# Softmax weights and q of two slots in two PSUM banks, six banks left for matmuls, GpSimd subtractions beside every large VectorE product, and the bound written by ScalarE

## The chip, the cores and the metric

The kernel runs on one core of a Trainium2 chip (trn2). The metric is the device time of one execution in microseconds; the median of three runs of the kernel before is 639.03 us.

## The reference

The input is one sequence of 2048 tokens with 640 features. Two branches of it are mixed by a gate per token.

```python
# A: 32 heads of 20 features, each token attends to 8 positions, 2 apart
logits = einsum("bhsd,bhswd->bhsw", q, k_gathered) * scale      # w = 8 offsets 0, 2, .., 14 back
logits = where(position >= 0, logits, -1e9)
a = (softmax(logits) @ v_gathered) @ wo
# B: 640 -> 1728 -> 640 with Mish between
b = mish(x @ w1 + b1) @ w2
g = sigmoid((x * gate_w).sum(-1))
out = g * a + (1 - g) * b
```

All is float32. Each float32 matrix is split into a high part (rounded to the type that TensorE multiplies, `fp32r`) and a low part (the rest), and a product is three matmuls: high by high, high by low, low by high.

## The kernel before, in words

**Stages on TensorE.** TensorE runs one fixed series: nine warm-up matmuls; eight units of q, k and v (`qkv`: a quarter of the heads and half of the tokens each, 8 slots of 15 matmuls) with the first MLP layer (`mlp1`: 52 tiles of 15 matmuls) between them; the second MLP layer (`mlp2`) as seven products a, b, c, e, g, d, f in Strassen's manner, each over seven blocks `kc` of the inner dimension; and `wo_out`, four token blocks of five output tiles. A product of `mlp2` has four to six output tiles ("p0", "u0" and so on, for two halves P), each with a PSUM bank of its own. Its first two and its last two blocks are done tile by tile: six matmuls for one tile, then six for the next.

**Splits.** Each operand is loaded into a staging buffer (`raw`, `hb`), ScalarE writes its high part (line 337), and VectorE or GpSimd subtracts it to give the low part (`low` in `split`, line 340). A `pair` holds both. TensorE waits for ScalarE before the first matmul of a pair, and for the subtracting engine before the second.

**Attention** runs on VectorE: for each two slots a product of q and the windows of k (line 424), a sum over the 20 features (line 427), the softmax (lines 442 to 452, with the exponential on ScalarE), then a product of weights `pw` and the windows of v (line 458) and sums (463, 464, 466). For the first tokens, which have positions before the start, GpSimd adds a bound of -BIG to one partition of the logits (line 435).

**What sets the order.** Nothing is issued as it comes. `Plan.run` plays all tasks through a list of assumed durations and writes the instructions of each engine in the order in which they start there; on the chip each engine works its list strictly in that order and waits at semaphores. Tasks marked "ANY" (most subtractions) may go to either engine. VectorE takes one only if it is due: if TensorE comes to it within `NEAR` = 8000 ns of the plan. GpSimd takes one while attention runs only if it ends within the time `quiet` in which VectorE does a large task of a certain kind, and is then bound by a wait (`follow`) to the VectorE instruction before that one. Before the change the kind is the sum "qk sum" alone (line 427). Banks of PSUM are handed out in a ring (`ps_buf`, 8 of them); a new tile takes the bank of the tile eight before it.

Of the kernel before, what the change touches and what calls it, by code (L numbers as in the profile page):

```python
# [26 lines left out]
BIG = 1e9  # L27
# [31 lines left out]
class Plan:  # L59
# [18 lines left out]
    def add(self, eng, ns, fn, after=(), rank=0.0, take=(), hold=(), size=0, kind="", late=0):  # L78
        t = Task(eng, ns, fn, rank, size / 330.0)
        t.kind, t.late = kind, late  # L80
        if eng == "POOL" and type(ns) is not tuple:
            t.ns = (ns, ns)
        for p in after:
            if p is not None:
                p.then.append(t)
                t.waits += 1
        t.take = list(take)
        t.hold = list(take) + [b for b in hold if b not in take]
        for b in t.hold:
            b.left += 1  # L90
        self.tasks.append(t)
        return t

    def run(self):
        ready = {e: [] for e in self.LAG}
# [33 lines left out]
        while left:  # L129
            again = not events or events[0][0] > now  # L130
            while again:
                again = False
                for e in self.LAG:
                    if busy[e]:
                        continue
                    fit = [t for t in ready[e] if fits(t)]
                    on = begun and loud
                    if e == "POOL":
                        fit += [t for t in shared if fits(t)]
                        if on:  # L140
                            fit = [t for t in fit if now + t.ns[0] <= quiet + 150 or t.rank < 0]
                    elif e == "DVE":
                        fit += [t for t in shared if fits(t) and (not on or due(t))]
                    if not fit:
                        continue
                    t = min(fit, key=lambda t: t.key)
                    if t.both:
                        shared.remove(t)
                        t.eng = e
                    else:  # L150
                        ready[e].remove(t)
                    if type(t.ns) is tuple:
                        t.ns = t.ns[e == "DVE"]
                    for b in t.take:
                        b.ring.free -= 1
                        b.ring.at += 1
                        b.t = b.make()
                    t.start = now
                    ins = t.fn(e) if t.both else t.fn()
                    if e == "POOL" and on and quiet > now and gate and ins:  # L160
                        self.follow(ins, gate)
                    if e == "DVE":
                        if t.kind:
                            begun = True
                            loud -= 1
                        if t.kind == "qk sum":
                            quiet, gate = now + t.ns, last
                        last = ins or last
                    if e == "PE":
                        begun_pe = max(begun_pe, t.pos)  # L170
                    busy[e] = again = True
                    end = over = now + t.ns * self.CARE.get(e, 1.0)
                    heapq.heappush(events, (over, n, "idle", e))
                    if t.land:
                        wire = max(wire, end) + t.land
                        end = wire + (0 if e == "SP" else self.ADDING)
# [36 lines left out]
def kernel(ctx: ExitStack, tc: tile.TileContext, x, wq, wo, w1, b1, w2, xt, gw, out):  # L213
    nc = tc.nc
    scale = DH ** -0.5
    V, G, A = nc.vector, nc.gpsimd, nc.scalar

    keep = ctx.enter_context(tc.tile_pool(name="keep", bufs=1))
    dram = ctx.enter_context(tc.tile_pool(name="dram", bufs=1, space=DRAM))
    psum = ctx.enter_context(tc.tile_pool(name="psum", bufs=8, space=PSUM))  # L220
    pe = ctx.enter_context(tc.tile_pool(name="pe", bufs=1, side="right"))
    at = ctx.enter_context(tc.tile_pool(name="at", bufs=1))

    NPAIR, NW, NRAW, NH = 21, 3, 7, 4
    def follow(ins, gate):
        tc.add_manual_dep(ins.ins, gate.ins.name,
                          mybir.DependencyInfo(mybir.DependencyClass.Sync, mybir.DependencyReason.DATA), reason="beside")

    plan = Plan({"bank": 8, "pair": NPAIR, "w": NW, "raw": NRAW, "raw1": 1, "hb": NH,
                 "ot": 1, "b": 11}, follow)  # L230

    def ps_buf():
        return plan.buf("bank", lambda: psum.tile([128, 512], F32, name="bank"))

    def pair_buf():
        return plan.buf("pair", lambda: pe.tile([128, 2, 512], F32R, name="pair", bufs=NPAIR))
# [34 lines left out]
    add = plan.add  # L271
# [5 lines left out]

    A.preload_act_table_set("mish")
    bias = keep.tile([128, FC + 1], F32)
    bound = keep.tile([1, 7, 7], F32)  # L280
    zt = keep.tile([128, 2, 8], F32)
    gate = keep.tile([128, 2, 8], F32)
    gc = keep.tile([128, 2, 8], F32)
# [18 lines left out]

    lg = at.tile([128, 8, HQ, W], F32, name="lg")
    lg_w = lg.rearrange("p s h w -> p s w h")
    pw = at.tile([128, 8, W, HQ], F32, name="pw")
    pr = at.tile([128, 2, W, QF], F32, name="pr")
    mx = at.tile([128, 8, HQ], F32, name="mx")
    sm = at.tile([128, 8, HQ], F32, name="sm")
# [15 lines left out]
    def consts_g():  # L324
        for i in range(2):
            G.memset(KV[i][0:1, 0:7], 0.0)

        G.memset(bound, 0.0)
        G.affine_select(bound, bound, pattern=[[1, 7], [1, 7]], compare_op=OP.is_ge,
                        fill=-BIG / scale, base=-7, channel_multiplier=0)  # L330

    cg = add("POOL", 5000, consts_g, rank=-1)


# [60 lines left out]
    def window(kv, s0, which):  # L395
        a = kv[:, s0:s0 + 9, which, :]
        return bass.AP(tensor=a.tensor, offset=a.offset, ap=[list(a.ap[0]), [ROW, 2], [ROW, W], [1, QF]])

    freed = {}
    spilled = {}  # L400
    att_end = {}
    shared_out = {}

    def attention(u, P, hq, ready, gates):


        kv, q = KV[UNIT[u]], Q[UNIT[u]]
# [13 lines left out]

        def scores(s0, rank, after):
            def mul():
                return V.tensor_tensor(pr, window(kv, s0, 0), q[:, s0:s0 + 2, None, :].to_broadcast([128, 2, W, QF]), op=OP.mult)  # L424

            def red():
                V.tensor_reduce(lg_w[:, s0:s0 + 2], pr.rearrange("p s w (h d) -> p s w h d", d=DH), op=OP.add, axis=AX.X)  # L427

            step = chain(rank)
            step("DVE", 2850, mul, ready[s0] + after, kind="qk")  # L430
            return step("DVE", 2750, red, kind="qk sum")

        def bounded(a, b, after):
            b = min(b, 7)
            return add("POOL", 3400, lambda: G.tensor_tensor(lg[0:1, a:b, :, 0:7], lg[0:1, a:b, :, 0:7],  # L435
                       bound[:, a:b, None, :].to_broadcast([1, b - a, HQ, 7]), op=OP.add), [cg] + after, rank=-1)

        def softmax(a, rank, after):

# [633 lines left out]
```

## Time and profile before

| | |
|---|---|
| three runs | 640.16, 639.03, 638.97 us; median 639.03 |
| profiled execution | span 636.9 us from its first to its last instruction; its time outside the span is not shown |
| TensorE busy | 631.9 us, 99% |
| VectorE busy | 584.1 us, 92% |
| ScalarE, GpSimd busy | 277.4 us, 215.2 us |

The median is 2.1 us longer than the span of the profiled execution, which is what starting and ending an execution takes outside it. The busy share of an engine is an average over stages; the list of waits says who ended the idle time of each engine, and the chain that ended last says which engine's work the end of the span hangs on.

### The profile page before, as it was taken

The numbers are of one execution on the slowest core, as the hardware profiler recorded it, in microseconds if no ns is written. First come the engines' busy times: TensorE is split into PE (matmuls) and PEld (weight loads), VectorE is DVE, ScalarE is ACT, GpSimd is POOL, SyncE is SP. The second block draws the span as 40 slices with busy tenths as digits, with TensorE's granted clock in tenths as the row PEclk, the third lists the DMA queues.
The fourth block names the chain that finished last, engine by engine and source line by source line (L and its number), as shares of the span: only waits on it lengthen the run. The fifth ranks groups of instructions, "written<-read, shape, count | busy, mean of one in ns | idle before, by whom it ended". The sixth has DMA issues, their size and how long they took to land.

```text
span 636.9 us, 8494 instructions
## 1 busy us (share of the span) xinstructions
PE 631.9 (99%) x2805; PEld 526.2 (83%) x2805; DVE 584.1 (92%) x584; ACT 277.4 (44%) x565; POOL 215.2 (34%) x157
## 2 busy tenths in 40 slices
PE   9999999999999999999999999999999999999997
PEld 6888888888888888888888888888888888888886
DVE  7888999999999999999899989799999999999941
ACT  7553353435436332542524244584676426721100
POOL 2212313131414442132343423204107328967310
PEclk9999999999999999999999999999999999999999
DMA  9999998867954994798499955989996758844642
GB/s 327 373 283 180 190 263 227 229 174 223 296 172 86 271 258 93 222 218 178 84 245 214 219 122 147 254 274 282 312 286 220 226 159 288 289 155 149 193 158 82
DMA packets 91323, 137.26 MB, mean 216 GB/s; under 512 B 12128, under 2 KB 41184, under 8 KB 91216
## 3 DMA queue, kind: packets, MB, share of 16 engines
q1 hardware_dynamic: 83600, 122.83, 62.6%
q0 software_dynamic: 7680, 13.90, 14.8%
q8 instruction: 22, 0.36, 0.2%
q14 instruction: 21, 0.17, 0.1%
HBM read 77.11 MB, written 57.81 MB: 212 GB/s over the span
## 4 chain that ended last, share of the span: by engine, by line
PE 99%; DVE 0%; issue 0%
PE bank L374 33%; PE bank L372 33%; PE bank L373 33%; PE bank L510 1%; PE bank L319 1%; DVE kvq L954 0%; DVE lg L315 0%
## 5 line engine op out<-in xcount | busy, mean ns | idle before, releaser
L372 PE MATMUL bank<-pair 128*128 128x512 f32 (+1 forms) x476 | 183.8, 386 | 0.0
L374 PE MATMUL bank<-pair 128*128 128x512 f32 (+1 forms) x476 | 183.7, 386 | 0.0
L373 PE MATMUL bank<-pair 128*128 128x512 f32 (+1 forms) x476 | 183.7, 386 | 0.0
L373 PEld LDWEIGHTS bank<-pair 128*128 128x128 f32 x476 | 89.3, 188 | 17.2
L374 PEld LDWEIGHTS bank<-pair 128*128 128x128 f32 x476 | 89.4, 188 | 17.1
L372 PEld LDWEIGHTS bank<-pair 128*128 128x128 f32 x476 | 89.3, 188 | 17.0
L424 DVE TENSOR_TENSOR pr<-kvq 128x2560 f32<-128x2560 f32 x32 | 90.8, 2839 | 3.5 <-DMA kvq<-kvq 1.6
L337 ACT ACTIVATE pair<-raw 128x512 fp32r<-128x512 f32 (+3 forms) x122 | 72.0, 615 | 48.4 <-DMA raw<-o 21.5
L458 DVE TENSOR_TENSOR pr<-kvq,pw 128x2560 f32<-128x2560 f32 x32 | 91.1, 2848 | 0.9
L427 DVE TENSOR_REDUCE lg<-pr 128x128 f32<-128x2560 f32 x32 | 90.2, 2818 | 0.6
L516 ACT ACTIVATE kvq<-bank 128x320 f32<-128x320 f32 x64 | 28.3, 442 | 114.7 <-PE bank L374 114.7
L435 POOL TENSOR_TENSOR lg<-lg,bound 1x168 f32<-1x168 f32 (+1 forms) x16 | 68.8, 4303 | 20.4 <-DVE lg L427 18.7
L625 ACT ACTIVATE hb<-bank,bias 128x512 f32<-128x512 f32 x52 | 35.9, 690 | 90.7 <-PE bank L374 77.2
L374 PE MATMUL bank<-pair,kvq 128*128 128x512 f32 (+1 forms) x188 | 72.6, 386 | 0.0
L372 PE MATMUL bank<-pair,kvq 128*128 128x512 f32 (+1 forms) x188 | 72.6, 386 | 0.0
L373 PE MATMUL bank<-pair,kvq 128*128 128x512 f32 (+1 forms) x188 | 72.6, 386 | 0.0
L340 POOL TENSOR_TENSOR pair<-raw,pair 128x496 fp32r<-128x496 f32 (+2 forms) x31 | 42.6, 1386 | 86.4 <-ACT pair L337 30.0
L372 PE MATMUL bank<-pair,w 128*128 128x512 f32 x182 | 70.8, 389 | 0.0
L373 PE MATMUL bank<-pair,w 128*128 128x512 f32 x182 | 70.8, 389 | 0.0
L374 PE MATMUL bank<-pair,w 128*128 128x512 f32 x182 | 70.8, 389 | 0.0
L340 DVE TENSOR_TENSOR pair<-raw,pair 128x512 fp32r<-128x512 f32 (+1 forms) x91 | 63.9, 721 | 5.2 <-ACT pair L337 5.2
L337 ACT ACTIVATE pair<-hb 128x512 fp32r<-128x512 f32 (+3 forms) x63 | 38.8, 615 | 42.7 <-DMA hb<-o 16.0
(89 smaller groups left out, 873.9 us busy)
## 6 DMA issues: line engine op xcount, KB each, us to landing
actt<-hb SPq DMA_DIRECT2D x52, 256.0 KB, 4.6
act<-hb SPq DMA_DIRECT2D x38, 256.0 KB, 4.6
raw<-actt SPq DMA_DIRECT2D x32, 256.0 KB, 4.5
raw<-act SPq DMA_DIRECT2D x29, 256.0 KB, 4.0
actt<-hb POOLq DMA_DIRECT2D x26, 256.0 KB, 6.2
actt<-actt POOLq DMA_DIRECT2D x24, 256.0 KB, 5.4
hb<-actt SPq DMA_DIRECT2D x24, 256.0 KB, 4.5
kvq<-in_xt SPq DMA_DIRECT2D x16, 320.0 KB, 7.2
```

Source lines behind the costliest of these rows:

```text
L319: nc.tensor.matmul(warm_bank.t, idle[:, :128], idle, start=True, stop=True)
L337: a = add("ACT", act_ns(n), lambda: A.activation(hi(), raw(), AF.Copy), after, rank=rank, take=take, hold=hold)
L340: return (V if e == "DVE" else G).tensor_tensor(lo(), raw(), hi().bitcast(F32), op=OP.subtract)
L372: nc.tensor.matmul(ps, ah, bh, start=first, stop=False, skip_group_check=more)
L373: nc.tensor.matmul(ps, ah, bl, start=False, stop=False, skip_group_check=more)
L374: nc.tensor.matmul(ps, al, bh, start=False, stop=last, skip_group_check=more)
L424: return V.tensor_tensor(pr, window(kv, s0, 0), q[:, s0:s0 + 2, None, :].to_broadcast([128, 2, W, QF]), op=OP.mult)
L427: V.tensor_reduce(lg_w[:, s0:s0 + 2], pr.rearrange("p s w (h d) -> p s w h d", d=DH), op=OP.add, axis=AX.X)
L435: return add("POOL", 3400, lambda: G.tensor_tensor(lg[0:1, a:b, :, 0:7], lg[0:1, a:b, :, 0:7], bound[:, a:b, None, :].to_broadcast([1, b - ...
L458: V.tensor_tensor(pr.rearrange("p s w (h d) -> p s w h d", d=DH), vw, pw[:, s0:s0 + 2, :, :, None].to_broadcast([128, 2, W, HQ, DH]), op=O ...
L516: a = add("ACT", 330, lambda: A.activation(kv[:, 7 + s], ps.t[:, QF:3 * QF].rearrange("p (a b) -> p a b", a=2), AF.Copy), [done] + before, ...
L625: a = add("ACT", 595, lambda: A.activation(to(it()), src(), AF.Mish, bias=bias[:n, fc:fc + 1]), after + [bias_in], rank=NEXT, take=[] if h ...
```

## The change

The weights `pw` and a copy `qs` of q for two slots each get a PSUM bank; ScalarE makes the copy (line 431 after) when the product before it has been done. So both large products of attention read one operand from PSUM and one from SBUF. Six banks are left for matmuls. The planner lets GpSimd work beside all three large kinds ("qk", "qk sum", "pv"). The bound is no longer added by GpSimd but written over the logits by ScalarE, slot by slot (line 440 after, 3 or 4 instructions where one was).

```diff
-                        if t.kind == "qk sum":
+                        if t.kind:
                             quiet, gate = now + t.ns, last
...
-    psum = ctx.enter_context(tc.tile_pool(name="psum", bufs=8, space=PSUM))
+    NBANK = 6
+    psum = ctx.enter_context(tc.tile_pool(name="psum", bufs=1, space=PSUM))
...
-        return plan.buf("bank", lambda: psum.tile([128, 512], F32, name="bank"))
+        return plan.buf("bank", lambda: psum.tile([128, 512], F32, name="bank", bufs=NBANK))
...
-    pw = at.tile([128, 8, W, HQ], F32, name="pw")
+    pw = psum.tile([128, 8, W, HQ], F32, name="pw")
+    qs = psum.tile([128, 512], F32, name="qs")[:, :2 * QF].rearrange("p (s f) -> p s f", f=QF)
...
-        G.memset(bound, 0.0)
-        G.affine_select(bound, bound, pattern=[[1, 7], [1, 7]], compare_op=OP.is_ge,
-                        fill=-BIG / scale, base=-7, channel_multiplier=0)
+        G.memset(bound, -BIG / scale)
...
-                return V.tensor_tensor(pr, window(kv, s0, 0), q[:, s0:s0 + 2, None, :].to_broadcast([128, 2, W, QF]), op=OP.mult)
+                return V.tensor_tensor(pr, window(kv, s0, 0), qs[:, :, None, :].to_broadcast([128, 2, W, QF]), op=OP.mult)
...
-            step("DVE", 2850, mul, ready[s0] + after, kind="qk")
+            c = add("ACT", 360, lambda: A.activation(qs, q[:, s0:s0 + 2], AF.Copy), ready[s0] + [asked[0]], rank=-1)
+            asked[0] = step("DVE", 2850, mul, [c] + after, kind="qk")
...
-            return add("POOL", 3400, lambda: G.tensor_tensor(lg[0:1, a:b, :, 0:7], lg[0:1, a:b, :, 0:7],
-                       bound[:, a:b, None, :].to_broadcast([1, b - a, HQ, 7]), op=OP.add), [cg] + after, rank=-1)
+            def run():
+                for s in range(a, b):
+                    A.activation(lg[0:1, s, :, 0:7 - s], bound[:, :, 0:7 - s], AF.Copy)
+            return add("ACT", 220 * (b - a), run, [cg] + after, rank=-1)
```

Since the planner's rule and its tasks change, the whole order is written anew. TensorE's list has the same matmuls in the same series, 924 of each of the three lines. Of the subtractions of line 340, VectorE had 165 and now has 120, GpSimd had 44 and now has 89. Lines 704, 808 and 821 (710, 814 and 827 after) share their tasks a little differently.

The first place is on VectorE where product c ends and product e begins. Line 808 (814 after) adds the four banks of c, one by one, to a kept tile; `pr` and `lg` belong to attention. Before:

```order
L340 TENSOR_TENSOR pair_4085<-raw_4013,pair_4085 128x512 [waits DMAHW5_49,PE_49,Activation_49]
L340 TENSOR_TENSOR pair_4102<-hb_4025,pair_4102 128x512 [waits DMAHW7_49,Activation_49]
L340 TENSOR_TENSOR pair_4108<-raw_4041,pair_4108 128x512 [waits DMAHW0_49,Activation_49]
L340 TENSOR_TENSOR pair_4119<-hb_4047,pair_4119 128x512 [waits DMAHW1_49,Activation_49]
L808 TENSOR_TENSOR kvq1_213<-kvq1_213,bank_3982 128x512 [waits PE_49]
L340 TENSOR_TENSOR pair_4122<-raw_4058,pair_4122 128x512 [waits DMAHW3_49,DMAHW2_49,Activation_49]
L340 TENSOR_TENSOR pair_4133<-raw_4088,pair_4133 128x512 [waits DMAHW4_49,Activation_49]
L808 TENSOR_TENSOR kvq1_213<-kvq1_213,bank_3999 128x512 [waits PE_49]
L340 TENSOR_TENSOR pair_4141<-hb_4091,pair_4141 128x512 [waits DMAHW5_49,Activation_49]
L808 TENSOR_TENSOR kvq1_213<-kvq1_213,bank_4017 128x512 [waits PE_49]
L808 TENSOR_TENSOR kvq1_213<-kvq1_213,bank_4034 128x512 [waits PE_49]
```

And the same place after:

```order
L425 TENSOR_TENSOR pr_218<-kvq2_3263,qs_217 128x2560
L340 TENSOR_TENSOR pair_4201<-raw_4073,pair_4201 128x512 [waits DMAHW2_49,DMAHW3_49,PE_49,Activation_49]
L340 TENSOR_TENSOR pair_4209<-raw_4082,pair_4209 128x512 [waits DMAHW4_49,PE_49,Activation_49]
L814 TENSOR_TENSOR kvq1_213<-kvq1_213,bank_4062 128x512 [waits PE_49]
L814 TENSOR_TENSOR kvq1_213<-kvq1_213,bank_4076 128x512 [waits PE_49]
L814 TENSOR_TENSOR kvq1_213<-kvq1_213,bank_4092 128x512 [waits PE_49]
L814 TENSOR_TENSOR kvq1_213<-kvq1_213,bank_4102 128x512 [waits PE_49]
L428 TENSOR_REDUCE lg_215<-pr_218 128x2x8x8 [waits DVE_49]
L340 TENSOR_TENSOR pair_4247<-raw_4114,pair_4247 128x512 [waits DMAHW6_49,Activation_49]
L340 TENSOR_TENSOR pair_4249<-hb_4166,pair_4249 128x512 [waits DMAHW5_49,Activation_49]
```

Before, the subtractions of the first blocks of e stand ahead of the four additions; now two of them stand behind the additions and behind a sum of attention.

The second place is TensorE's list at the same point: the last matmul of c and the first ones of e, the second of which (pair_4247, pair_4108 before) is block `kc` = 1 for the first tile. Before:

```order
L374 MATMUL bank_4034<-pair_4068,pair_4038 128x512
L372 MATMUL bank_4183<-pair_4085,pair_4076 128x512 [waits Activation_49]
L373 MATMUL bank_4183<-pair_4085,pair_4076 128x512 [waits DVE_49]
L374 MATMUL bank_4183<-pair_4085,pair_4076 128x512
L372 MATMUL bank_4183<-pair_4108,pair_4076 128x512 [waits Activation_49]
L373 MATMUL bank_4183<-pair_4108,pair_4076 128x512 [waits DVE_49]
```

And after:

```order
L374 MATMUL bank_4102<-pair_4195,pair_4097 128x512
L372 MATMUL bank_4234<-pair_4209,pair_4201 128x512 [waits Activation_49]
L373 MATMUL bank_4234<-pair_4209,pair_4201 128x512 [waits DVE_49]
L374 MATMUL bank_4234<-pair_4209,pair_4201 128x512
L372 MATMUL bank_4234<-pair_4247,pair_4201 128x512 [waits Activation_49]
L373 MATMUL bank_4234<-pair_4247,pair_4201 128x512 [waits DVE_49]
```

TensorE's series has not moved; the wait for VectorE in the last row is five matmuls behind the last matmul of c in both.

The third place is GpSimd in the first quarter of the program, where weights of q, k and v (128x496) are split; line 613 (619 after) is a DMA that adds to a block in DRAM. Before:

```order
L613 DMA actt_1_1_127<-hb 128x512 [waits DMAHW3_49,Activation_49]
L340 TENSOR_TENSOR pair<-raw,pair 128x496 [waits DMAHW6_49,DVE_49]
L340 TENSOR_TENSOR pair<-raw,pair 128x496 [waits DMAHW7_49,Activation_49]
L613 DMA actt_0_2_121<-hb 128x512 [waits DMAHW4_49,Activation_49]
L613 DMA actt_1_2_128<-hb 128x512 [waits DMAHW7_49,Activation_49]
L340 TENSOR_TENSOR pair<-raw,pair 128x496 [waits DMAHW0_49,DVE_49]
L340 TENSOR_TENSOR pair<-raw,pair 128x496 [waits DMAHW2_49,PE_49]
L435 TENSOR_TENSOR lg<-lg,bound 1x24x7 [waits DVE_49]
```

And after:

```order
L340 TENSOR_TENSOR pair<-raw,pair 128x496 [waits DMAHW3_49,DVE_49,Activation_49]
L340 TENSOR_TENSOR pair<-raw,pair 128x496 [waits DMAHW4_49,Activation_49]
L619 DMA actt_1_1_127<-hb 128x512 [waits DMAHW0_49,Activation_49]
L340 TENSOR_TENSOR pair<-raw,pair 128x496 [waits DVE_49,DMAHW5_49,PE_49,Activation_49]
L710 TENSOR_TENSOR raw<-raw 128x256 [waits DMAHW7_49,DMAHW1_49,Pool_49]
L340 TENSOR_TENSOR pair<-raw,pair 128x496 [waits DVE_49,DMAHW2_49,PE_49,Activation_49]
L340 TENSOR_TENSOR pair<-raw,pair 128x496 [waits DMAHW5_49,PE_49,Activation_49]
```

All five subtractions of this quarter's weights are now GpSimd's, with the adding DMAs between them, and the addition of the bound is gone from its list.

More of the change, by code (lines that the diff above doesn't have):

```diff
@@ L227, in follow @@
                           mybir.DependencyInfo(mybir.DependencyClass.Sync, mybir.DependencyReason.DATA), reason="beside")
-    plan = Plan({"bank": 8, "pair": NPAIR, "w": NW, "raw": NRAW, "raw1": 1, "hb": NH,
+    plan = Plan({"bank": NBANK, "pair": NPAIR, "w": NW, "raw": NRAW, "raw1": 1, "hb": NH,
                  "ot": 1, "b": 11}, follow)
     def ps_buf():
-        return plan.buf("bank", lambda: psum.tile([128, 512], F32, name="bank"))
+        return plan.buf("bank", lambda: psum.tile([128, 512], F32, name="bank", bufs=NBANK))
     def pair_buf():
@@ L279 @@
     bias = keep.tile([128, FC + 1], F32)
-    bound = keep.tile([1, 7, 7], F32)
+    bound = keep.tile([1, HQ, 7], F32)
     zt = keep.tile([128, 2, 8], F32)
@@ L399 @@
     freed = {}
+    asked = [None]
     spilled = {}
```

## The prediction

> **What bounds the kernel now.** I read the page first: busy times, the clock row, and the chain that ended last.
>
> ```profile
> PE 631.9 (99%) x2805; PEld 526.2 (83%) x2805; DVE 584.1 (92%) x584; ACT 277.4 (44%) x565; POOL 215.2 (34%) x157
> PEclk9999999999999999999999999999999999999999
> PE 99%; DVE 0%; issue 0%
> ```
>
> TensorE is busy for 631.9 us of a span of 636.9 at a full clock, and the chain is TensorE's nearly alone. A busy engine may still be spaced out by waits, so the list of waits for TensorE comes next, and then the end of the timeline.
>
> ```profile
> PE bank L319 <- DVE lg L315: 1.2, 1, 1.2
> ...
> 632.52 0.39 PE L373 MATMUL bank<-pair,kvq 128*128 128x512 f32 x1
> 632.74 0.39 PE L374 MATMUL bank<-pair,kvq 128*128 128x512 f32 x1
> 633.17 0.69 DVE L954 TENSOR_TENSOR kvq<-bank,kvq 128x512 f32<-128x512 f32 x1 [2.71 <-PE bank L374]
> 633.89 0.33 SPq L346 DMA_DIRECT2D out<-kvq  x1
> ```
>
> In the whole span TensorE waits once, for 1.2 us before its first matmul. From there it runs without a gap to 632.74. What lies outside is those 1.2 us and some 4 us at the end: the last addition and the last transfer. So there is nothing to win on TensorE: every microsecond that VectorE saves is saved beside TensorE, and every microsecond for which TensorE is made to wait is added to the end whole, since no gap can take it up. The question is only whether the new order makes it wait.
>
> **The change part by part.** First the engines beside TensorE. These rows, from the groups with shapes kept apart, price the moved work.
>
> ```profile
> L340 DVE TENSOR_TENSOR pair<-raw,pair 128x512 fp32r<-128x512 f32 x76 | 54.7, 736 | 5.2 <-ACT pair L337 5.2
> L340 POOL TENSOR_TENSOR pair<-raw,pair 128x512 fp32r<-128x512 f32 x13 | 18.3, 1413 | 36.4 <-ACT pair L337 21.1 <-DVE pr L424 11.5 <-DVE pair L340 3.8
> L435 POOL TENSOR_TENSOR lg<-lg,bound 1x224 f32<-1x224 f32 x8 | 42.9, 5358 | 19.1 <-DVE lg L427 17.6 <-PE bank L374 1.6
> L435 POOL TENSOR_TENSOR lg<-lg,bound 1x168 f32<-1x168 f32 x8 | 26.0, 3248 | 1.2 <-DVE lg L427 1.1
> L516 ACT ACTIVATE kvq<-bank 128x320 f32<-128x320 f32 x64 | 28.3, 442 | 114.7 <-PE bank L374 114.7
> L520 ACT ACTIVATE hx<-bank 128x16 f32<-128x16 f32 x64 | 12.7, 198 | 0.0
> ```
>
> VectorE loses 45 subtractions: 45 x 0.736 = 33 us, so some 551 us stay of 584.1. GpSimd gains them at 45 x 1.413 = 64 us and loses the bound, 42.9 + 26.0 = 69 us: no change in sum. ScalarE gains 32 copies of 320 elements, 32 x 0.442 = 14 us, and 56 short writes at 0.198 us, 11 us: 302 us. None of these comes near TensorE's 631.9, so as sums they cost nothing. If their cover were gone, it would have to be by a delay at one place.
>
> The large products keep their length if an operand in PSUM costs what one in SBUF costs. Additions of the same size with and without a bank show it:
>
> ```profile
> L808 DVE TENSOR_TENSOR kvq<-kvq,bank 128x512 f32<-128x512 f32 x8 | 5.3, 672 | 0.0
> L808 DVE TENSOR_TENSOR kvq<-kvq 128x512 f32<-128x512 f32 x4 | 2.6, 677 | 0.0
> ```
>
> 672 against 677 ns: nothing, so both products stay at their present length. A gain of those 5 ns on 64 products would be 0.3 us; a loss, were it even 0.1 us each, 6.4 us, and both lie beside TensorE.
>
> **The ring of six banks.** In the stages with q, k and v a tile takes 15 matmuls of about 0.227 us (632.52 to 632.74, and finer 469.54 to 469.77 below), 3.4 us, so the bank of the tile six before it has five tiles, 17 us, to be read out. ScalarE reads it, and its longest hold-up is here:
>
> ```profile
> 70.95 0.66 ACT L628 ACTIVATE hb<-hb 128x512 f32<-128x512 f32 x1
> 76.22 0.74 ACT L337 ACTIVATE w<-raw 128x640 fp32r<-128x640 f32 x1 [4.61 <-DMA raw<-in_w]
> 79.82 0.62 ACT L337 ACTIVATE pair<-raw 128x496 fp32r<-128x496 f32 x1 [2.85 <-DMA raw<-in_wq]
> 80.34 0.42 ACT L516 ACTIVATE kvq<-bank 128x320 f32<-128x320 f32 x1
> ```
>
> No bank is read from 71 to 80.3 us, 9.4 us, which fits into 17. ScalarE's new instructions are a new wait, too: the copy of q waits for the product before, the bound for a sum, and behind them stand the readers of banks and the high parts. Such a wait is at most one VectorE product, 2.8 us, and fits as well: 9.4 + 2.8 = 12.2. I take nothing here. In `mlp2` tiles are finished 6 x 0.227 = 1.36 us apart, and the third tile of e, the first to reuse a bank of c, starts five such steps, 6.8 us, after that bank is full; the additions that empty them stand directly in turn, so nothing here either.
>
> **The place that costs.** I followed each subtraction of the new order from TensorE's wait back through its engine's list to the last instruction ahead of it that itself waits for a late matmul. One place fails, where product c ends. These are the matmuls and the VectorE rows there before.
>
> ```profile
> 469.54 0.39 PE L374 MATMUL bank<-pair 128*128 128x512 f32 x1
> 469.77 0.39 PE L372 MATMUL bank<-pair 128*128 128x512 f32 x1
> ...
> 466.52 0.69 DVE L340 TENSOR_TENSOR pair<-raw,pair 128x512 fp32r<-128x512 f32 x1
> 470.73 1.28 DVE L808 TENSOR_TENSOR kvq<-kvq,bank 128x512 f32<-128x512 f32 x2
> ```
>
> The matmul at 469.54 is the last of c. The fifth after it, at 469.54 + 5 x 0.227 = 470.67, needs the low part of the second pair of e. Before, that subtraction ran at 466.52 and was done at 467.21, 3.5 us early, and the fourth addition of c's banks came long after it. In the new order the same subtraction (pair_4247) stands behind the four additions and behind a sum of attention (line 428), and the fourth addition waits for that last matmul. So TensorE waits for a chain that its own matmul starts:
>
> ```profile
> 527.84 2.81 DVE L427 TENSOR_REDUCE lg<-pr 128x128 f32<-128x2560 f32 x1
> 530.57 0.68 DVE L340 TENSOR_TENSOR pair<-hb,pair 128x512 fp32r<-128x512 f32 x1
> ...
> 89.08 2.83 DVE L424 TENSOR_TENSOR pr<-kvq 128x2560 f32<-128x2560 f32 x1 [1.06 <-DMA kvq<-kvq]
> 92.00 2.47 POOL L340 TENSOR_TENSOR pair<-raw,pair 128x496 fp32r<-128x496 f32 x2 [13.22 <-DVE pr L424]
> ```
>
> From the start of the matmul to the addition: 633.17 - 632.74 = 0.43 us, as at the end of the span. The addition: 0.60, half the distance from 470.73 over two of them. The sum of attention: 530.57 - 527.84 = 2.73. The subtraction: 0.68. From its end to the engine that waits: 92.00 - 91.91 = 0.09, by the GpSimd row that waited for a product. Together 4.53 us. Of these TensorE covers five matmuls, 1.13 us. It waits 4.53 - 1.13 = 3.4 us. Lower end 3.1 (no hand-over time, a slightly shorter start); upper end 4.5, if VectorE comes a little late to its first addition. The next subtraction (pair_4249) is wanted 12 matmuls later, 2.7 us, and is done 0.6 us after the first: no second wait.
>
> Behind the place nothing takes the 3.4 us back, as TensorE has no gap. Everything beside it only gets that much more time. The other parts being nothing, the span becomes 636.9 + 3.4 = 640.3, and with the 2.1 us that lie around the span of the profiled execution, 642.4, which is 0.5% above the median of 639.03. A measurement of this kernel tells about 0.2%, 1.28 us, from no change.
>
> **The rivals.** *A second wait, on GpSimd's list.* Twice as many subtractions stand there now, with the adding DMAs of line 613 among them.
>
> ```profile
> POOL actt L613 <- DMA actt<-actt: 45.8, 9, 7.6
> POOL actt L613 <- ACT hb L625: 20.7, 3, 11.4
> ```
>
> The longest single holds are 7.6 and 11.4 us. A subtraction that is 3.5 us early, as the one above, and is held by 7.6, costs 4.1: 646.5. For it: GpSimd takes 1.41 us where VectorE takes 0.74. Against: before, 44 subtractions stood in that list and none made TensorE wait, and these adding DMAs are mostly over before `mlp2`, where the margins are short. The Trainium skill's GPSIMD Engine Reference (Engine selection) advises VectorE for elementwise work on two inputs, since GpSimd is about 2x slower there; the ratio 1413 to 736 agrees. That rule speaks against the change and raises this rival's chance, no more. I give it 0.2, together with a late load at the place above, which would give 643 to 646.
>
> *The products shut GpSimd out after all.* GpSimd stands still beside VectorE instructions with two SBUF operands; here beside a product and sums, while an addition with a bank passes:
>
> ```profile
> 530.79 25.72 POOL L435 TENSOR_TENSOR lg<-lg,bound 1x224 f32<-1x224 f32 x1 [0.47 <-DVE lg L427]
> ...
> 570.52 6.37 POOL L821 TENSOR_TENSOR kvq<-kvq,w 128x512 f32<-128x512 f32 x2
> 573.16 0.68 DVE L954 TENSOR_TENSOR raw<-bank,raw 128x512 f32<-128x512 f32 x1
> 573.76 1.98 DVE L463 TENSOR_TENSOR pr<-pr 128x1280 f32<-128x1280 f32 x1
> ```
>
> An addition with a bank took 0.68 us beside GpSimd, its length alone. If the new products did hold GpSimd up, each of the 45 would cost VectorE up to one GpSimd instruction, 1.41 us, 64 us in all: 551 + 64 = 615, still under TensorE, but with subtractions late by up to 2.8 us, more than some margins allow; half a dozen such waits give 642.4 + 6 x 2.8 = 659. The Trainium skill's page SBUF — State Buffer (Who interferes with whom) says that a VectorE instruction with at most one SBUF input does not contend with GpSimd; by that rule this rival falls away, and the row at 573.16 agrees. Chance 0.05.
>
> *Not slower.* The wait does not bind because the subtraction gets done before the sum of attention has begun: the point is that it must be finished by 1.13 us after the last matmul of c. That would be so if TensorE's wait there counted an earlier VectorE instruction than the one that I read from the names. Then all is under cover and the time is 639.0. What speaks for it is that the planner meant the order to flow; against it, the names and each engine's fixed order. Chance 0.08. A real gain would need TensorE's 1.2 us at the start or the end's 4 us to shrink, which no edit touches: 0.01.
>
> **How the numbers follow.** The forecast, 3.1 to 4.5 us of waiting at that one place and no other of weight, has 0.66. It gives 642.1 to 643.5, most likely 642.4. With GpSimd or the load (0.2) the time is 643 to 646.5, with the shut-out (0.05) up to 659, without a wait (0.08) 639.0. To leave out no more than 0.2, the range reaches from 641.7 to 646.8: it leaves out the not slower cases, the shut-out, and a little of the second. Faster by over 0.2%: 0.01; within 0.2%: 0.08; slower: 0.91.
>
> **What would show it.** Right: in the profile after, TensorE's waits list line 373 waiting for VectorE's pair of line 340, some 3.4 us, at about 470 us, with line 428 running ahead of it, and no other wait of a microsecond; VectorE near 550 us, subtractions nearer to 0.69 than 0.74 without the bound in the way; both products near 2.83 us beside GpSimd's subtractions at 1.3. Wrong: TensorE without a wait there, or the largest wait elsewhere, by GpSimd's list, ScalarE or a bank; or GpSimd's subtractions stretched to 3 us and more while a product runs.

## The result, and the profile after

The kernel after takes 648.17 us (median of four runs, 644.47 to 649.23), the one before 639.0 (638.97 to 640.16). The ratio is 1.0128, with a 95% interval of 1.0110 to 1.0145: slower by 9.2 us, where the prediction has 3.4 and a range that ends at 646.8.

The page of the profile after (span 646.7 us): busy times, the clock row, and the chain that ended last.

```profile
PE 636.0 (98%) x2805; PEld 528.7 (82%) x2805; DVE 559.5 (87%) x534; ACT 290.4 (45%) x651; POOL 205.2 (32%) x190
PEclk9999999999999999999999999999989999999999
PE 88%; DVE 6%; DMA 2%; issue 2%; POOL 0%; SPq 0%; DVEq 0%; POOLq 0%
```

VectorE, ScalarE and GpSimd moved about as worked out. But the chain now runs through VectorE for 6% of the span, and the clock row, flat before, has an 8. The waits for TensorE after say where:

```profile
PE bank L373 <- DVE pair L340: 5.7, 2, 3.2
PE bank L321 <- DVE lg L317: 1.2, 1, 1.2
```

Two waits where one was forecast, together 5.7 us, while the span grew by 9.8. The rest is seen in TensorE's timeline after (start, length of one):

```profile
470.97 0.39 PE L372 MATMUL bank<-pair 128*128 128x512 f32 x1
474.56 0.79 PE L373 MATMUL bank<-pair 128*128 128x512 f32 x1 [3.20 <-DVE pair L340]
475.15 0.63 PE L374 MATMUL bank<-pair 128*128 128x512 f32 x1
475.58 0.63 PE L372 MATMUL bank<-pair 128*128 128x512 f32 x1
...
477.63 0.40 PE L374 MATMUL bank<-pair 128*128 128x512 f32 x1
...
559.47 0.39 PE L372 MATMUL bank<-pair 128*128 128x512 f32 x1
562.39 0.50 PE L373 MATMUL bank<-pair 128*128 128x512 f32 x1 [2.54 <-DVE pair L340]
```

Starts that follow each other at 0.227 us everywhere else are 3.59 us apart at 470.97 (3.36 too many) and 2.92 at 559.47 (2.70 too many). Behind the first wait the matmuls start 0.43 us apart until 477.63: TensorE works at about half its clock. Such a row of slow matmuls is called a slow stretch below, and its cost is the time by which its starts take longer than usual. From 474.56 to 477.63 seven starts take 3.07 us where 1.59 is usual: 1.48 us. Behind the second wait the same stretch costs 1.72 us. The clock also came up later at the start of this execution. TensorE's timeline before, then after, where the nine warm-up matmuls stand ahead:

```profile
4.80 3.43 PE L510 MATMUL bank<-pair,kvq 128*128 128x496 f32 x13
```

```profile
1.21 4.02 PE L321 MATMUL bank<-lg 128*128 128x512 bf16 x9 [1.21 <-DVE lg L317]
4.75 3.57 PE L516 MATMUL bank<-pair,kvq 128*128 128x496 f32 x11
```

Eleven matmuls in 3.57 us where 13 took 3.43, which is 0.6 us. It need not be an effect of the change: the kernel with the planner's old rule, below, loses 0.3 us more there in its trace, and has the time of before. The sum is 3.36 + 2.70 + 1.48 + 1.72 + 0.6 = 9.9 us, the whole difference between the two profiled spans. Of the four runs after, the shortest (644.47) is the one with a mean granted clock of 1.000; the others have 0.995.

The first wait is the predicted one. These are VectorE's rows at that place after: the fourth addition, the sum of attention, the subtraction.

```profile
470.49 0.69 DVE L814 TENSOR_TENSOR kvq<-kvq,bank 128x512 f32<-128x512 f32 x1 [0.67 <-PE bank L374]
471.09 2.81 DVE L428 TENSOR_REDUCE lg<-pr 128x128 f32<-128x2560 f32 x1
473.82 0.68 DVE L340 TENSOR_TENSOR pair<-raw,pair 128x512 fp32r<-128x512 f32 x1
```

The second is at product f, where VectorE adds and gates the results of d (lines 814 and 827). The two timelines after, VectorE first, then GpSimd:

```profile
546.02 0.84 DVE L380 STREAM_TRANSPOSE ot<-kvq 128x640 f32<-128x640 f32 x1
...
552.58 1.67 DVE L827 TENSOR_TENSOR kvq<-kvq,w 128x512 f32<-128x512 f32 x1
554.17 1.78 DVE L814 TENSOR_TENSOR kvq<-kvq,raw 128x512 f32<-128x512 f32 x1
555.98 0.69 DVE L814 TENSOR_TENSOR kvq<-kvq 128x512 f32<-128x512 f32 x1
...
557.19 1.78 DVE L827 TENSOR_TENSOR kvq<-kvq,w 128x512 f32<-128x512 f32 x1
558.89 1.77 DVE L814 TENSOR_TENSOR kvq<-kvq 128x512 f32<-128x512 f32 x1
560.59 1.75 DVE L340 TENSOR_TENSOR pair<-hb,pair 128x512 fp32r<-128x512 f32 x1
```

```profile
550.37 5.02 POOL L827 TENSOR_TENSOR kvq<-kvq,w 128x512 f32<-128x512 f32 x3
556.90 1.53 POOL L340 TENSOR_TENSOR pair<-hb,pair 128x512 fp32r<-128x512 f32 x1 [1.50 <-ACT pair L337]
558.46 3.33 POOL L340 TENSOR_TENSOR pair<-raw,pair 128x512 fp32r<-128x512 f32 x2
```

A VectorE instruction takes 0.68 us where GpSimd has no work (555.98) and 1.7 us where it has. So the subtraction at 560.59, the last in the row, is late. The Trainium skill (SBUF — State Buffer, Who interferes with whom) says that a VectorE instruction with two SBUF inputs contends with a GpSimd instruction that reads SBUF; these rows agree, and give the price. The first row says why GpSimd is loose here: it is the last of attention. The same row of before stands 49 us later:

```profile
595.19 0.83 DVE L380 STREAM_TRANSPOSE ot<-kvq 128x640 f32<-128x640 f32 x1
```

The planner holds GpSimd back only while attention runs; strictly, in its own time, until it issues attention's last large instruction, which starts at 532.0 us after and at 578.1 before. Relieved of 45 subtractions, VectorE was through with attention before product f began, and the restraint had ended. That the one follows from the other is put to the test below.

### The profile page after: what moved, and what is told of

The parts are those of the page before. It is cut to its first block, busy times and chain, and to the rows that moved or that the text cites. A ratio compares the mean times of both kernels' runs of the same rounds, so it can differ in the third digit from the quotient of the medians.

```text
span 646.7 us, 8607 instructions
## 1 busy us (share of the span) xinstructions
PE 636.0 (98%) x2805; PEld 528.7 (82%) x2805; DVE 559.5 (87%) x534; ACT 290.4 (45%) x651; POOL 205.2 (32%) x190
## 4 chain that ended last, share of the span: by engine, by line
PE 88%; DVE 6%; DMA 2%; issue 2%; POOL 0%; SPq 0%; DVEq 0%; POOLq 0%
PE bank L373 29%; PE bank L374 29%; PE bank L372 29%; DVE pair L340 3%; DVE kvq L814 1%; DMA raw<-actt 1%; PE bank L516 1%; DMA b<-raw 1%; PE bank L321 1%; DVE pr L469 0%; DMA hb<-actt 0%; DVE pr L470 0%; POOL pair L340 0%; SPq L346 0%; DVE kvq L827 0%
## 5 line engine op out<-in xcount | busy, mean ns | idle before, releaser
L340 POOL TENSOR_TENSOR pair<-raw,pair 128x512 fp32r<-128x512 f32 (+2 forms) x54 | 71.3, 1337 | 140.9 <-ACT pair L337 76.9
L425 DVE TENSOR_TENSOR pr<-kvq,qs 128x2560 f32<-128x2560 f32 x32 | 90.2, 2817 | 13.4 <-ACT qs L431 12.3
L340 DVE TENSOR_TENSOR pair<-raw,pair 128x512 fp32r<-128x512 f32 (+2 forms) x68 | 51.8, 781 | 7.7 <-ACT pair L337 7.7
L469 DVE TENSOR_TENSOR pr<-pr 128x1280 f32<-128x1280 f32 x32 | 50.8, 1589 | 0.9
```

Source lines behind the costliest of these rows:

```text
L340: return (V if e == "DVE" else G).tensor_tensor(lo(), raw(), hi().bitcast(F32), op=OP.subtract)
L425: return V.tensor_tensor(pr, window(kv, s0, 0), qs[:, :, None, :].to_broadcast([128, 2, W, QF]), op=OP.mult)
L469: step("DVE", 1495, lambda: V.tensor_tensor(pr[:, :, 0:4], pr[:, :, 0:4], pr[:, :, 4:8], op=OP.add))
```

## The experiments

Theory: the first wait is one of order; the second comes from GpSimd beside VectorE; each costs its length and a stretch at half clock. The rivals: the slow matmuls come from something else at those places; the second wait is a late load or high part; or the parts of the change (operands in PSUM, six banks, ScalarE's bound) cost in themselves. Each kernel's median stands beside that of before in the same session (639.1 to 639.4).

| kernel | us | ratio to before (95%) |
|---|---|---|
| first place cured | 644.64 | 1.0086 (1.0071 to 1.0101) |
| second place cured | 647.31 | 1.0119 (1.0102 to 1.0137) |
| both cured | 645.00 | 1.0081 (1.0068 to 1.0094) |
| first wait filled with matmuls | 645.54 | 1.0099 (1.0084 to 1.0114) |
| planner's old rule, all else new | 639.37 | 1.0007 (0.9998 to 1.0017) |
| bound by GpSimd, all else new | 650.34 | 1.0176 (1.0161 to 1.0192) |
| planner's cost of the exponential | 644.92 | 1.0084 (1.0068 to 1.0101) |
| the same, GpSimd quiet after attention | 638.89 | 0.9996 (0.9986 to 1.0005) |
| new rule alone, all else old | 659.03 | 1.0305 (1.0286 to 1.0324) |

### The two places, one by one

The written order is kept, and single instructions are issued later: at the first place the fourth addition goes behind the late subtraction and the sum behind the other subtractions; at the second, four of GpSimd's instructions go behind its next three subtractions.

```diff
+    plan.later[marks["c", 1, 1]] = low_of(E, 1, 1)
+    plan.later[marks["sum", 7, 2]] = marks["pv", 7, 6]
```

```diff
+    plan.later.update({("POOL", i): 174 for i in range(167, 171)})
```

> The kernel after, with VectorE's list changed at the first place alone: the subtraction that TensorE waits for stands ahead of the fourth addition of c, and the sum of attention behind the other subtractions of e. Theory (a wait costs its own length and then a slow stretch of TensorE's clock): the wait of 3.36 us and the 1.48 us by which the next seven matmuls are long both go, 648.2 - 4.8 = 643.4 us; the wait of 2.5 us at 560 us stays, with its slow stretch. Rival A (the long matmuls come from something else at that place, such as late operands or loads): only the 3.36 us go, 644.8. Rival C (the wait is only moved to the next pair of e): 646 to 648.

> The kernel after, with four instructions of GpSimd (one line 814, three line 827, planned at 549 to 554 us) put behind its next three subtractions; nothing else moves. Theory (the second wait comes from VectorE instructions that take 1.7 us instead of 0.68 beside GpSimd): VectorE's lines 814 and 827 at 549 to 556 us take 0.68 us, the subtraction is done some 5 us earlier, the wait of 2.70 us and its slow stretch of 1.72 us go: 648.2 - 4.4 = 643.8 us. Rival B (the subtraction waits for its load or for ScalarE's high part): no change, 648.2. Rival D (the four, now later, collide with the subtractions behind them and make a new wait): 645 to 648, with TensorE's wait between 562 and 575 us.

> Both cures together. Theory: TensorE is without a wait again and the time is that of the kernel before, 639.0 us (to 639.6, since the clock came up 0.6 us later at the start of the profiled execution after). If a third cause was hidden below the two: more than 640.5 us. If what VectorE was relieved of were worth something once the waits are gone: below 638.

Measured: 644.64, 647.31 and 645.00. The first lies nearer to rival A (644.8) than to the theory (643.4), so the time alone does not support the theory; the trace decides. The long wait is gone, and no slow stretch is left at either place, but there are eight short waits now: four between 470 and 508 us, where the long one had given VectorE time, and four at 557 to 567. TensorE's list with the first place cured:

```profile
PE bank L387 <- DVE pair L354: 3.7, 8, 0.7
```

By the starts, which count the slower first matmul behind each wait too, the eight cost 6.0 us, nearly all of the 6.5 us by which this span is longer than that of before.

With the second place cured, the rows that took 1.7 us do take 0.7 (GpSimd is idle there), and the subtraction is done before 557 us instead of at 562. VectorE's timeline of that kernel (its line 354 is the subtraction, 830 is 814):

```profile
555.62 0.68 DVE L830 TENSOR_TENSOR kvq<-kvq 128x512 f32<-128x512 f32 x1
556.22 0.68 DVE L354 TENSOR_TENSOR pair<-hb,pair 128x512 fp32r<-128x512 f32 x1
```

The mechanism of the second wait is shown. The time, however, falls only by 0.9 us where 4.4 were expected: in the profiled execution the first wait was 4.2 us long in TensorE's list (4.4 by the starts), with a slow stretch of 2.3, and a new wait near 579 us costs 0.7. The other three runs left no trace. Up to there its lists are those of the kernel after, yet its product before the first place (line 425 after, 440 here) starts at 465.88 us where after has 463.99:

```profile
465.88 2.81 DVE L440 TENSOR_TENSOR pr<-kvq,qs 128x2560 f32<-128x2560 f32 x1
```

In two more kernels with the same lists up to there (first place cured, first wait filled) it starts at 465.11 and 464.78: VectorE's lateness differs by up to 2 us between executions, and what makes it differ stays open. With both cured five waits for a pair remain, the longest of 1.2 us, and one of 0.4 for an addition, together 5.2 us by the starts, and the time is 645.0 us instead of the expected 639. As these lists read, the two waits had been hiding a shortage on VectorE behind them, and taking them away one at a time opens the next.

### The clock

The filled wait repeats the first three matmuls of e, so that TensorE works until the subtraction is done.

```diff
+                            if name == "e" and first[key] and key == ("w", 0, 0):
+                                for _ in range(5):
+                                    mm3(..., True, False, True)
```

> The kernel after, with TensorE kept busy in the first wait: the first three matmuls of product e are done six times instead of once (15 more matmuls, 3.40 us, each round starting its bank anew), so that they end when the subtraction does. The wait in time stays, the idleness goes. Theory (the clock falls because TensorE stands idle): the next matmuls are spaced 227 ns again, 648.2 - 1.5 = 646.7 us. Rival A (late operands or loads at that place): the spacing stays at 427 ns, and the time at 648.2 or a little above.

Measured: 645.54. The subtraction comes as late as ever, and yet behind it matmuls start 0.30, 0.24 and then 0.23 us apart, as TensorE's timeline of that kernel shows:

```profile
474.55 0.39 PE L372 MATMUL bank<-pair 128*128 128x512 f32 x1
474.77 0.46 PE L373 MATMUL bank<-pair 128*128 128x512 f32 x1
475.07 0.40 PE L374 MATMUL bank<-pair 128*128 128x512 f32 x1
475.31 0.39 PE L372 MATMUL bank<-pair 128*128 128x512 f32 x1
```

So it is TensorE's own idleness that halves the clock, not what the operands wait for. The 1.1 us below the expected 646.7 come from the second place, whose waits were shorter in this execution (2.1 us in two) and had no slow stretch. Then waits of known length, put into the kernel before:

```diff
+            if place in WAITS:
+                nc.tensor.matmul(ps.t, W1[fc].t[:, 0, 0], X[tb, 0].t[:, 0], start=True, stop=True)
+                for _ in range(WAITS[place]):
+                    A.activation(gap[:, :16], ps.t[:, :16], AF.Copy)
```

> The kernel before, with 16 waits of known lengths put into TensorE's series in the first MLP layer, three tiles or more apart: a matmul, then 2, 4, 7, 10, 13, 16, 20 or 28 short reads of its bank by ScalarE (each length twice), then the tile, which begins with the same matmul again. The 16 more matmuls are 3.6 us; 200 reads of about 0.2 us and 16 times 0.3 us are some 45 us of waiting. Rival A (a wait costs its own length and nothing else): 639 + 3.6 + 45 = 688 us, every matmul after a wait at 227 ns. Theory (after a long wait TensorE's clock is halved for some 3.4 us): each wait of 3 us and more is followed by some eight matmuls at 427 ns, 1.6 us; waits of 1 us and less by none; 8 of the 16 long ones give 688 + 13 = 701 us, and the granted clock of the run is below 1.

> The kernel before with 16 waits again, now all between 2.6 and 3.4 us long (11 to 15 short reads by ScalarE). If the clock falls by a threshold on the length of the wait alone, between the 3.02 us that it bore twice and the 3.66 us that it did not bear, then each length is followed by slow matmuls always or never. If it falls by what a fixed grid of windows sees (the 2.70 us in the kernel after were followed by a slow stretch), then it is a matter of chance, with a share that rises from a few in ten at 2.6 us to nearly all at 3.4 us. The sum of the waits is some 48 us: 639 + 3.6 + 48 = 691 us, and 1.5 to 3 us more for each slow stretch.

Measured: 707.45 us where 701 was expected, and 717.14 where 691 and the stretches were. A wait here is the distance of two matmul starts less 0.227 us; the table counts the places with a wait of each length, and those where matmuls 0.43 us apart, a slow stretch, followed:

| wait, us | 0.65 to 2.37 | 2.59 | 2.80 | 3.02 | 3.23 | 3.45 | 3.66 to 6.24 |
|---|---|---|---|---|---|---|---|
| places | 8 | 3 | 3 | 6 | 3 | 3 | 6 |
| with a slow stretch | 0 | 2 | 3 | 2 | 2 | 3 | 6 |

Two of them in TensorE's timeline of the first of these kernels, a wait of 3.66 us and one of 3.02:

```profile
50.78 0.39 PE L668 MATMUL bank<-pair,w 128*128 128x512 f32 x1
54.67 0.79 PE L374 MATMUL bank<-pair,w 128*128 128x512 f32 x1 [3.50 <-ACT gap L670]
55.26 0.63 PE L375 MATMUL bank<-pair,w 128*128 128x512 f32 x1
...
162.13 0.39 PE L668 MATMUL bank<-kvq,w 128*128 128x512 f32 x1
165.38 0.50 PE L374 MATMUL bank<-kvq,w 128*128 128x512 f32 x1 [2.85 <-ACT gap L670]
165.72 0.39 PE L375 MATMUL bank<-kvq,w 128*128 128x512 f32 x1
```

Up to 2.4 us a wait costs its length and 0.11 us, as the matmul behind it takes 0.34 us to the next start. From 3.66 us on the slow stretch always follows. Between, it came at 12 of 18 places, and at 3.02 us both ways, so the length alone does not decide. A stretch begins at once or up to 1.6 us after the wait and costs 1.6 to 3.0 us, 2.1 in the mean of 18. It thus comes at one place and not at the next, as if by chance, and the 644.47 us among the four runs agrees with two waits without slow stretches, though no trace of that run shows it. The Trainium skill (TensorE: Matmul & The Clock Gate, The HAM clock gate) tells of a gate that watches windows of some 3.4 us in a grid of its own, and of half clock after at least one idle window. The chance and the delayed onset agree with such a grid; that a whole window must be idle does not, since 2.59 us sufficed at two of three places.

### The parts of the change

The old rule in the new kernel, the old bound in the new kernel, and the new rule in the old kernel:

```diff
-                        if t.kind:
+                        if t.kind == "qk sum":
                             quiet, gate = now + t.ns, last
```

> The kernel after, with the planner's rule of before: GpSimd may work only beside the sum of line 428. Operands in PSUM, six banks and the bound by ScalarE stay; the order is planned anew. Theory (the second wait comes because VectorE, relieved of subtractions, ends attention some 27 us earlier, so that GpSimd is let loose before product f begins): VectorE is back near 575 to 585 us, attention ends later than 560 us, and there is no wait at 560 us; whether the first place recurs is a matter of the order: 639.0 without it, 643.5 with it. Rival (operands in PSUM, six banks or ScalarE's additional work cost in themselves): above 645 us with waits for banks or for ScalarE in TensorE's list.

Measured: 639.37, the time before, and no wait but that at the start. Operands in PSUM, six banks and ScalarE's new work cost nothing. Attention's last row starts at 595.89 us again, and GpSimd stands idle for 30 us at the place in question, without any bound in its list. GpSimd's timeline of that kernel:

```profile
571.00 1.29 POOL L340 TENSOR_TENSOR pair<-hb,pair 128x512 fp32r<-128x512 f32 x1 [29.98 <-DVE sm L455]
```

```diff
-                    A.activation(lg[0:1, s, :, 0:7 - s], bound[:, :, 0:7 - s], AF.Copy)
+            return add("POOL", 3400, lambda: G.tensor_tensor(lg[0:1, a:b, :, 0:7], lg[0:1, a:b, :, 0:7],
```

> The kernel after, with the bound added by GpSimd again (one instruction for four slots, line 435 of before); the rule for all three kinds, PSUM operands and six banks stay; the order is planned anew. Theory (before, the long bound held GpSimd for 25 us at the end of attention and so kept it away from VectorE): GpSimd is held again some time around 505 to 530 us, and the place at 560 us depends on whether attention is over; VectorE near 551 us, so GpSimd is loose there and the wait remains if it is not in a bound: 645 to 650 us. Rival (GpSimd's bound was what hindered it, and its removal is what matters): GpSimd's subtractions come late behind bounds of 3 to 25 us and TensorE waits several times more, 655 us and above.

Measured: 650.34, just above the range that the theory gave, with 7.6 us of waits near 470 and 562 us. But its reason fell: the bound does not hold GpSimd. It takes 0.82 us instead of 5.36 in the groups of this kernel, so it is no shield there:

```profile
L440 POOL TENSOR_TENSOR lg<-lg,bound 1x224 f32<-1x224 f32 x8 | 6.5, 816 | 20.3 <-DVE lg L430 20.2
```

```diff
-                        if t.kind == "qk sum":
+                        if t.kind:
```

> The kernel before, with the planner's new rule alone: GpSimd may work beside all three large kinds, whose operands are both in SBUF still; eight banks, bound by GpSimd. If products with two SBUF operands stand in GpSimd's way as sums do with bounds, GpSimd's subtractions beside them take about as long as the product, 2.5 to 3 us, and VectorE's instructions behind them wait: TensorE waits several times, 645 to 665 us. If they do not, the operands in PSUM are worth nothing: 639 to 645.

Measured: 659.03. With both operands of the products in SBUF GpSimd's subtraction takes 2.49 us on the average, in the kernel after 1.40; the product of q and k is longer too (2.87 against 2.82), and TensorE waits nine times for a pair. The groups and waits of the kernel with the rule alone, then the groups after:

```profile
L424 DVE TENSOR_TENSOR pr<-kvq 128x2560 f32<-128x2560 f32 x32 | 91.7, 2865 | 0.4
L340 POOL TENSOR_TENSOR pair<-raw,pair 128x512 fp32r<-128x512 f32 x27 | 67.1, 2491 | 65.6 <-ACT pair L337 28.4 <-DVE pw L452 12.0 <-DVE lg L443 10.3
PE bank L373 <- POOL pair L340: 9.8, 6, 2.8
PE bank L373 <- DVE pair L340: 1.9, 3, 0.9
```

```profile
L425 DVE TENSOR_TENSOR pr<-kvq,qs 128x2560 f32<-128x2560 f32 x32 | 90.2, 2817 | 13.4 <-ACT qs L431 12.3
L340 POOL TENSOR_TENSOR pair<-raw,pair 128x512 fp32r<-128x512 f32 x33 | 45.9, 1399 | 59.8 <-ACT pair L337 33.7 <-DMA raw<-act 7.1 <-DVE kvq L472 5.4
```

So the operands in PSUM do what they are for: they make the rule bearable, 648 instead of 659 us. The bound does not explain these 11 us, as the kernel above has GpSimd's bound again and takes 650. The rule itself is what costs.

### Both causes cured in the planner

The planner assumes 2.94 us for the exponential on ScalarE; the trace shows 1.28 us for loading its table and 0.42 us of work. ScalarE's timeline after:

```profile
465.24 1.28 ACT L450 ACT_TABLE_LOAD   x1
466.54 0.42 ACT L450 ACTIVATE lg<-lg 128x256 f32<-128x256 f32 x1
```

ScalarE also writes the high parts, so in the planner's time the one for the late subtraction seems to have come only after the sum; this is argued from the planner's durations, and the first edit is the test. The second edit keeps the planner's restraint up after attention. It holds for both engines: GpSimd may work only beside large instructions, and VectorE takes only subtractions that are due.

```diff
-            return add("ACT", 360 + 2 * TABLE, lambda: A.activation(lg[:, h], lg[:, h], AF.Exp, ...
+            return add("ACT", 360 + TABLE, lambda: A.activation(lg[:, h], lg[:, h], AF.Exp, ...
```

```diff
-                    on = begun and loud
+                    on = begun
```

> The kernel after, with one number of the planner changed: the exponential of the softmax is assumed at 1.65 us instead of 2.94 (the trace shows one table load of 1.28 us and 0.42 us of work). In its own time the planner then writes an order without the gap of 5.06 us that it had foreseen on TensorE where c ends and e begins. Theory (the first wait is written into this one order, not into the parts of the change; the second comes from GpSimd beside VectorE's instructions with two SBUF operands after the end of attention, which the planner does not know): no wait near 470 us; waits of 1 to 4 us in all may remain between 545 and 580 us, 639.5 to 643.5 us. Rival (VectorE's relief by the rule brings TensorE's waits in any order): 644 us and above.

> As the run before it, and GpSimd may work only beside the large instructions after the end of attention too (so not at all there, but for its urgent tasks). Theory: neither wait is left, and the time is that of the kernel before, 639.0 to 639.7 us. If VectorE alone is now too slow at the end: more than 641, with waits after 560 us. If the change gives anything once its two waits are gone: below 638.3.

Measured: 644.92 with the first edit alone, 638.89 with both. The first lies above the theory's 643.5, where the rival has it (waits in any order, 644 and above), and it takes the second edit to refute that rival. With the first, the wait near 470 us is gone; one wait is left, behind the matmul at 555.75 us, 4.02 us by the starts, with a slow stretch of 2.8. VectorE stands in 1.7 us rows there again, beside GpSimd's. The two timelines of that kernel, VectorE and GpSimd:

```profile
547.38 3.48 DVE L814 TENSOR_TENSOR kvq<-kvq 128x512 f32<-128x512 f32 x2
```

```profile
548.57 1.74 POOL L814 TENSOR_TENSOR kvq<-kvq,raw 128x512 f32<-128x512 f32 x1
```

With the second edit GpSimd has no instruction from 540 to 570 us, VectorE's row of the same kind takes half as long, and TensorE waits for nothing but its start. VectorE's timeline and TensorE's waits of that kernel:

```profile
549.21 1.28 DVE L814 TENSOR_TENSOR kvq<-kvq 128x512 f32<-128x512 f32 x2
PE bank L321 <- DVE lg L317: 1.2, 1, 1.2
```

So the first edit does not suffice and the two together do, in an order planned anew; the second alone was not run. It is no gain on before either, though VectorE has 30 us less to do (554.1 us): TensorE has no gap to give.

## Why the prediction was wrong

**What bounds the kernel: right.** No version has a median below 638.9 us, and each wait of TensorE shows in the end.

**The sums beside TensorE: right within 12 us.** VectorE 559.5 for 551, ScalarE 290 for 302, GpSimd 205 for 210. VectorE's subtractions were expected nearer to 0.69 than 0.74 us; those from `raw` take 0.81 on the average. The rows near 560 us suggest why, GpSimd's own work beside them; it is the term that the working missed.

**PSUM operand, six banks, ScalarE's waits at nothing: right.** Both products take 2.82 us, beside GpSimd too, and the kernel with the old rule has the time of before.

**The place that costs: right.** 3.36 us by the starts for 3.4, in the row, behind the instructions and at the time that were named.

**"No other of weight": the step that failed.** The working followed each subtraction back to an instruction that waits for a late matmul. That finds waits of order alone; the VectorE instructions in between were taken at their lengths of before, 0.68 us, and no wait was looked for that comes from their getting longer. In before's trace GpSimd did nothing but a bound for 25.7 us at that time, and attention ran until 595. The working saw that VectorE loses 33 us but not that attention then ends sooner, nor that the planner's restraint on GpSimd ends with it. Before's trace had the price: three subtractions and a gating at 560 to 565 us took 1.2 us each as soon as GpSimd ran beside them, at 560.59. VectorE's timeline of before:

```profile
560.04 2.39 DVE L340 TENSOR_TENSOR pair<-raw,pair 128x512 fp32r<-128x512 f32 x2
```

The second wait is 2.70 us. The rival of a second wait (0.2) foresaw one, of 4.1 us, but for another reason: GpSimd's list was not late, it slowed VectorE's.

**"Added to the end whole": mis-sized.** A wait of 3.4 us costs 3.36 + 1.48 here, and 2.1 us on top in the mean of the known waits that had a slow stretch. The flat clock row of before could not show it, but the nine warm-up matmuls at its start hinted at it: they took 4.02 us, 0.45 us each. The two slow stretches together are 3.2 us, a third of the difference.

**"Everything beside it only gets more time": right, and it matters.** With the first wait cured, four short ones come up at once in its place.

**The products shut GpSimd out (0.05): right to be refused for this kernel,** and its price of 659 us is, by chance, what the rule alone gives without operands in PSUM.

## What to carry to other kernels

Where one engine bounds a kernel without a gap, relief of another engine gains nothing by itself (30 us off VectorE gave none here) and can cost: look for the waits that a new order writes, and price each as its length plus a slow stretch of the clock once it comes near 2.6 us, the shortest that brought one here. When work is taken from an engine, ask which later phase then begins sooner and which rule or cover ends with the old one; durations taken from a stretch in which a neighbour was silent do not hold when it is let loose. And a wait that is cured alone shows the next one; the cause is tested by an order that has none.

## What the runs showed that was not expected

TensorE's clock halves after some waits of 2.6 to 3.5 us and not after others of the same length (12 of 18 places), never up to 2.4 and always from 3.7, for 1.6 to 3.0 us of loss each. Behind a wait without a slow stretch the first matmul still takes 0.11 us more. The small product that writes the weights takes 0.43 us when it writes to PSUM; the rows of before and of after:

```profile
L452 DVE TENSOR_TENSOR pw<-lg,sm 128x256 f32<-128x256 f32 x16 | 11.6, 723 | 0.5
```

```profile
L458 DVE TENSOR_TENSOR pw<-lg,sm 128x256 f32<-128x256 f32 x16 | 6.9, 433 | 0.5
```

One instruction of 1.72 us at 567.83, beside GpSimd, lifts the mean of before; by the medians, 0.66 and 0.43 us, writing to PSUM saves 0.22 us in each of 16, off the path. What decides whether a wait of 2.6 to 3.5 us brings the slow clock at one place and not at the next stays open.
